# One load for the modulation weights, and TensorE's loop body in seven marked parts with branch hints, in a decode kernel

## The chip, the cores and the metric

The kernel runs on one core of a Trainium2 chip. The metric is the device time of one execution in microseconds. For the kernel before it is the median of three runs. A profile of one execution gives the span from its first to its last instruction, the busy time of each engine and every DMA packet.

## What is computed

A decode step (one token for each of B = 8 sequences, width D = 512) of a block with adaptive layer norm, attention over a key and value cache, and a dense layer:

```
mod = silu(c) @ w_mod                       # 512 x 3072; six parts sa, ca, ga, sb, cb, gb
h = layernorm(x) * (1 + ca) + sa
q = h @ wq                                  # 32 heads of 128
o = softmax(q k^T / sqrt(128)) v            # 8 key/value heads, 8192 positions, per sequence
x = x + ga * (o @ wo)
h = layernorm(x) * (1 + cb) + sb
x = x + gb * (relu(h @ w1 + b1)^2 @ w2 + b2)   # width 1792
```

All inputs are bfloat16. The key and value caches hold 8 x 8 x 8192 x 128 elements each, 134 MB each; everything is read once.

## The kernel before, in words

**The units of the caches.** The caches are read in units of two heads of one sequence, 4 MB each: 128 partitions of 32 KB. A sequence has four key units and four value units, so there are 64 units. They go through `RING`, four slots in SBUF; unit n uses slot n mod 4. `load(n)` (L354 to L367) issues a unit's DMA on SyncE's queue once the slot's last reader, a matmul of TensorE, has run; the last value unit goes in four pieces (L362).

**The start.** SyncE issues, in this order: w_mod into slot 2 (L288, two DMAs: partitions 0 to 15, then 16 to 127), wq into slot 3 (L290), key units 0 and 1 into slots 0 and 1 (L367), the two biases (L451, L452), wo (L453), then key units 2 and 3 as soon as TensorE has read w_mod and wq out of their slots. ScalarE's queue brings c (L284) and x (L285). GpSimd builds constants (L297 to L344). TensorE transposes silu(c) (L375), x (L381) and the normalised x (L394), multiplies by w_mod (L400, 24 matmuls of 512 columns), turns the result (L414, L423), and multiplies the modulated `haT` by wq (L400 again, 32 matmuls). `haT` is written by VectorE after L414.

**The loop.** One pass per sequence, eight passes. A pass does, for each of the four key units and each quarter k of it: 32 transposes of 128 x 128 tiles on TensorE (L481), copies of the results out of PSUM by VectorE (L488) and ScalarE (L486), and eight score matmuls of the quarter before (L498). Then the row maximum, the exponential (L564), the turning of the probabilities (L576), and for each value unit 32 matmuls (L618), a copy (L628) and four small matmuls (L632). A few matmuls on constants (L465, L471) write banks that nobody reads afterwards.

**Who writes the order.** `op` and `dma` append to one list per engine, in the order of the Python text. `Prog._looped` (L126 to L154) writes the list of TensorE, VectorE and ScalarE: first what stands ahead of the loop, then a hardware loop of `passes` passes whose body is written once, with part "a" of every pass and part "b" of all but the last, then what comes after. SyncE's and GpSimd's lists are written out in full. A wait stands in front of an instruction where a token has not been seen by its engine. Part "a" of TensorE's list is numbered j = 0, 1, 2, ... in `_looped`; that number counts matmuls.

**The end.** After the last pass come the output projection (L525, L706), the second layer norm, w1 (L739) and w2 (L753), whose weights are the last loads on SyncE's queue (L659, L661), and the output (L761, L769).

The two DMAs of w_mod, as they stand:

```
wmod_p = w_mod.rearrange("(p k) n -> p (k n)", k=KT)
for a, z in ((0, 16), (16, 128)):
    d_wm = dma("sync", s_wm, lambda e, a=a, z=z: e.dma_start(
        RING[a:z, 2, 0:KT * NMOD], wmod_p[a:z]))
d_wq = dma("sync", s_wq, lambda e: e.dma_start(
    RING[:, 3, :], A_wq.rearrange("(p k) n -> p (k n)", k=KT)))
```

Of the kernel before, what the change touches and what calls it, by code (L numbers as in the profile page):

```python
# [12 lines left out]
class Tok:  # L13
# [4 lines left out]
    def __init__(self, op, at, sem=None, val=None):  # L18
        self.op, self.at, self.sem, self.val = op, at, sem, val


class Op:
# [3 lines left out]
    def __init__(self, eng, fn, deps, sem, at):  # L26
        self.eng, self.fn, self.deps, self.sem, self.at = eng, fn, [d for d in deps if d is not None], sem, at
        self.tok, self.users = None, set()
        for d in self.deps:
            if d.op is not None:  # L30
                d.op.users.add(eng)


class Prog:
# [25 lines left out]
    def dma(self, eng, sem, fn, deps=()):  # L60
        self.dma_n[sem] = self.dma_n.get(sem, 0) + 16
        self.ops[eng].append(Op(eng, fn, deps, sem, self.at))
        return Tok(None, self.at, sem, self.dma_n[sem])
# [61 lines left out]

    def _looped(self, e, eng, passes):  # L126
        nc, per, pe = self.nc, self.per[e], self.LOOP[e]
        seen, first = {}, {}
        for o in self._part(e, None):
            self._emit(eng, o, self._want(e, o, 0), seen)  # L130
        for i in range(passes):
            for p in "ab":
                for j, o in enumerate(self._part(e, (i, p))):
                    want = self._want(e, o, i)
                    inside = {s: v for s, v in want.items() if s in per}
                    assert all(v <= per[s] for s, v in inside.items())
                    assert all(d.at is None or d.sem in per for d in o.deps), (e, i, p, j)
                    assert first.setdefault((p, j), inside) == inside, (e, i, p, j)
                    self._emit(eng, None, {s: v for s, v in want.items() if s not in per}, seen)
        with nc.Fori(0, passes, engines=[pe], head_slot={pe: 0} if e == "tensor" else None) as i:  # L140
            self.batch = i
            for j, o in enumerate(self._part(e, (0, "a"))):
                self._emit(eng, o, first["a", j], seen)
            after = dict(seen)
            with eng.If(i < passes - 1):
                for j, o in enumerate(self._part(e, (0, "b"))):
                    self._emit(eng, o, first["b", j], seen)
                self._emit(eng, None, per, seen)
                eng.drain()
                for s, n in per.items():  # L150
                    eng.sem_inc(s, -n)
            self.batch = None
        for o in self._part(e, "post"):
            self._emit(eng, o, self._want(e, o, passes - 1), after)  # L154
# [14 lines left out]
def bass_adaLN_cond__gqa_block_cached__dense_activation_squared_relu__decode_kernel(  # L169
# [6 lines left out]
    NMOD = w_mod.shape[1]  # L176
    KT = D // 128
# [9 lines left out]
    with ExitStack() as es:  # L187
        E = es.enter_context
        sb = lambda name, shape, dt: E(nc.sbuf_tensor(name, shape, dt))
        RING = sb("ring", [128, NSLOT, UNIT], BF16)  # L190
# [80 lines left out]
        op, dma = Pg.op, Pg.dma  # L271
        sem = lambda name: E(nc.semaphore(name))
        s_c, s_x, s_wm, s_wq, s_wo, s_bb = (
            sem(f"d_{n}") for n in ("c", "x", "wm", "wq", "wo", "bb"))
# [8 lines left out]

        d_c = dma("scalar", s_c, lambda e: e.dma_start(c_sb, c))  # L284
        d_x = dma("scalar", s_x, lambda e: e.dma_start(x_sb, A_x.rearrange("b s d -> (b s) d")))  # L285
        wmod_p = w_mod.rearrange("(p k) n -> p (k n)", k=KT)
        for a, z in ((0, 16), (16, 128)):
            d_wm = dma("sync", s_wm, lambda e, a=a, z=z: e.dma_start(  # L288
                RING[a:z, 2, 0:KT * NMOD], wmod_p[a:z]))
        d_wq = dma("sync", s_wq, lambda e: e.dma_start(  # L290
            RING[:, 3, :], A_wq.rearrange("(p k) n -> p (k n)", k=KT)))

# [238 lines left out]
        for b in range(B):  # L531
# [5 lines left out]
            for p in range(NP):  # L537
                n = 2 * NP * b + p
# [69 lines left out]
            for p in range(NP):  # L608
                if p == NP - 1:
                    Pg.at = "post" if lastb else (b, "b")  # L610
                n = 2 * NP * b + NP + p
# [191 lines left out]
```

## Time and profile before

| what | value |
|---|---|
| median of three runs | 675.81 us (675.12 to 675.97) |
| the profiled execution's own time | 675.12 us |
| its span, first to last instruction | 673.3 us |
| TensorE matmul busy | 517.4 us, 77% of the span |
| TensorE weight load busy | 347.1 us, 52% |
| VectorE busy | 302.5 us, 45% |
| ScalarE busy | 258.9 us, 38% |
| GpSimd busy | 18.6 us, 3% |
| moved by DMA | 283.85 MB, mean 422 GB/s |
| mean granted TensorE clock | 0.888 |

How to read it. Times of single rows come from the profiled execution, whose own time is 1.8 us longer than its span. In the page, the rows of 40 digits cut the span into 40 equal slices (16.8 us each) and give the busy share of an engine in tenths, 9 for 90% or more. A DMA's landing time runs from its issue to the arrival of its completion. In a row of waits, "A <- B: total, times, longest" means that engine and line A stood idle until B was done. "q1" is the queue of SyncE's DMAs, "q10" that of ScalarE's, and a row of kind "instruction" counts DMA packets that bring program code, here in pieces of 16 KB on "q8" and smaller ones on "q14".

### The profile page before, as it was taken

To read this page: it belongs to the slowest core of one execution; us is meant where nothing else is said; L and a number is where in the kernel's file an instruction comes from. 1 tells how busy PE (TensorE), PEld (TensorE's weight loads), DVE (VectorE), ACT (ScalarE), POOL (GpSimd) and SP (SyncE) were. 2 spreads that over 40 slices of the span, in tenths; PEclk is the share of its full clock that TensorE was granted. 3 is DMA by queue.
4 is the path that set the end of the run, shared out by engine and by line. 5 is a ranking of instruction groups with operands and counts; after the bars stand their busy time and mean duration, and the time that the engine had idled before them with its cause. 6 is when DMAs were issued, how large, how long until landed. Compare 5 with 4: busy or idle time off the path is not lost.

```text
span 673.3 us, 15486 instructions
## 1 busy us (share of the span) xinstructions
PE 517.4 (77%) x7064; PEld 347.1 (52%) x7064; DVE 302.5 (45%) x571; ACT 258.9 (38%) x289; POOL 18.6 (3%) x76
## 2 busy tenths in 40 slices
PE   0684986699839986599756998399856998489886
PEld 0373742577318752377316763187424773177534
DVE  1242551367315662267414663066612674156622
ACT  2143560265404661166403662056601664046610
POOL 7300000000000000000000000000000000000000
PEclk9778898699977999699977999789995999689995
DMA  9999999999999999999999999999999999999996
GB/s 233 425 414 434 433 424 433 434 434 432 424 434 432 430 436 432 432 430 428 432 430 436 432 434 432 426 432 428 436 432 434 432 426 432 430 434 432 434 413 265
DMA packets 12192, 283.85 MB, mean 422 GB/s; under 512 B 1266, under 2 KB 1299, under 8 KB 3604
## 3 DMA queue, kind: packets, MB, share of 16 engines
q1 hardware_dynamic: 12132, 283.65, 99.1%
q8 instruction: 9, 0.15, 0.1%
q10 hardware_dynamic: 48, 0.02, 0.0%
q14 instruction: 3, 0.02, 0.0%
HBM read 283.66 MB, written 0.01 MB: 421 GB/s over the span
## 4 chain that ended last, share of the span: by engine, by line
PE 52%; DMA 37%; ACT 7%; DVE 2%; SPq 1%; issue 1%
PE PS L481 36%; DMA ring<-in_A_k_cache_dram 32%; PE PS L498 9%; ACT P_sb L564 5%; DMA ring<-in_A_wq_dram 3%; DMA ring<-in_B_w_dram 2%; PE PS L618 2%; PE PS L471 1%; ACT KTb L486 1%; SPq L661 1%; DVE O_sb L628 1%; PE PS L465 1%; PE PS L576 1%; DVE Pm L590 0%; PE PS L596 0%
## 5 line engine op out<-in xcount | busy, mean ns | idle before, releaser
L486 ACT ACTIVATE KTb<-PS 128x1024 bf16<-128x1024 bf16 x192 | 196.7, 1024 | 331.2 <-PE PS L481 331.2
L481 PE MATMUL PS<-IDENT,ring 128*128 128x128 bf16 x4096 | 269.5, 228 | 49.7 <-DMA ring<-in_A_k_cache_dram 49.7
L481 PEld LDWEIGHTS PS<-IDENT,ring 128*128 128x128 bf16 x4096 | 248.8, 103 | 98.5 <-DMA ring<-in_A_k_cache_dram 50.9
L488 DVE COPY KTb<-PS 128x1024 bf16<-128x1024 bf16 x320 | 210.1, 687 | 145.3 <-PE PS L481 143.1
L618 PE MATMUL PS<-ring,Pm 128*32 128x512 bf16 x992 | 70.8, 435 | 45.3 <-DMA ring<-in_A_v_cache_dram 44.3
L498 PE MATMUL PS<-KTb,Qb 128*32 128x512 bf16 x1024 | 79.2, 386 | 4.5 <-ACT KTb L486 4.5
L628 DVE CAST O_sb<-PS 128x512 bf16<-128x512 f32 x31 | 21.4, 692 | 125.5 <-PE PS L618 125.5
L618 PEld LDWEIGHTS PS<-ring,Pm 128*32 128x32 bf16 x992 | 26.9, 106 | 83.8 <-DMA ring<-in_A_v_cache_dram 52.1
L564 ACT ACTIVATE P_sb<-PS,negm 128x1024 bf16<-128x1024 f32 x32 | 35.2, 1112 | 20.2 <-DVE negm L559 20.2
L471 PE MATMUL PS<-ONES 128*128 128x512 f32 x80 | 42.1, 630 | 0.0
L576 PE MATMUL PS<-IDENT,P_sb 128*128 128x128 bf16 x256 | 19.9, 220 | 15.4 <-ACT P_sb L564 15.4
L590 DVE COPY Pm<-PS 64x512 bf16<-64x512 bf16 x48 | 20.2, 421 | 25.0 <-PE PS L576 24.6
L576 PEld LDWEIGHTS PS<-IDENT,P_sb 128*128 128x128 bf16 x256 | 14.4, 98 | 25.2 <-ACT P_sb L564 25.2
L465 PE MATMUL PS<-IDENT 128*128 128x512 bf16 x88 | 26.9, 380 | 0.0
L498 PEld LDWEIGHTS PS<-KTb,Qb 128*32 128x32 bf16 x1024 | 15.4, 94 | 21.1 <-ACT KTb L486 8.5
L505 DVE TENSOR_REDUCE m<-PS 128x1 f32<-128x512 f32 x32 | 22.0, 689 | 6.6 <-PE PS L498 6.6
L632 PEld LDWEIGHTS PS<-SEL,O_sb 128*128 128x128 bf16 x124 | 5.8, 98 | 30.8 <-DVE O_sb L628 30.8
L471 PEld LDWEIGHTS PS<-ONES 128*128 128x128 f32 x80 | 12.7, 190 | 10.6 <-issue 10.6
L632 PE MATMUL PS<-SEL,O_sb 128*128 128x8 bf16 x124 | 7.9, 169 | 12.4 <-DVE O_sb L628 12.0
L400 PE MATMUL PS<-ring,KTb 128*32 128x512 bf16 x56 | 7.2, 626 | 7.8 <-DMA ring<-in_w_mod_dram 4.6
L643 DVE TENSOR_TENSOR oTn<-PS,rinv 128x8 f32 x31 | 6.0, 194 | 14.9 <-PE PS L632 14.9
L465 PEld LDWEIGHTS PS<-IDENT 128*128 128x128 bf16 x88 | 7.7, 105 | 9.1 <-issue 7.2
(132 smaller groups left out, 120.0 us busy)
## 6 DMA issues: line engine op xcount, KB each, us to landing
ring<-in_A_k_cache_dram SPq DMA_DIRECT2D x32, 4096.0 KB, 34.2
ring<-in_A_v_cache_dram SPq DMA_DIRECT2D x31, 4096.0 KB, 27.4
ring<-in_A_wq_dram SPq DMA_DIRECT2D x1, 4096.0 KB, 25.0
wo_sb<-in_A_wo_dram SPq DMA_DIRECT2D x1, 4096.0 KB, 53.4
ring<-in_w_mod_dram SPq DMA_DIRECT2D x1, 2688.0 KB, 15.7
ring<-in_A_v_cache_dram SPq DMA_DIRECT2D x1, 2048.0 KB, 23.5
ring<-in_B_w_dram SPq DMA_DIRECT2D x3, 512.0 KB, 17.6
ring<-in_B_w_dram SPq DMA_DIRECT2D x1, 1344.0 KB, 18.8
```

The source lines that it names most:

```text
L465: ts = [op("tensor", lambda e: e.matmul(bank(at).rearrange("p (a r) -> p a r", a=4), IDENT[:, :], rhs)) for _ in range(n)]
L471: ts = [op("tensor", lambda e: e.matmul(bank(at).rearrange("p (a r) -> p a r", a=4), ONES[:, :], rhs)) for _ in range(n)]
L481: t = op("tensor", lambda e, j=j, i=i: e.matmul(STG[j][:, i, :], src[:, 32 * k + 8 * j + i, :], IDENT[:, :], is_transpose=True), [loaded[n ...
L486: stg_free[j] = op("scalar", lambda e, j=j, dst=dst: e.activation(dst, STG[j], ACT.Copy), [t])
L488: stg_free[j] = op("vector", lambda e, j=j, dst=dst: e.tensor_copy(dst, STG[j]), [t])
L498: t = op("tensor", lambda e, hf=hf, q=q, rhs=rhs: e.matmul(PS[32 * q:32 * (q + 1), k, :], Qb[:, 2 * p + hf, :], rhs, start=(p == 0 and hf ...
L505: return op("vector", lambda e: e.tensor_reduce(m4[:, k:k + 1], bank(k), AX.X, ALU.max), [t])
L564: exps.append(op("scalar", lambda e, k=k: e.activation(P_sb[:, k, :, :, :], bank(k).rearrange("p (i x) -> p i x", i=8).unsqueeze(2).to_bro ...
L576: t = op("tensor", lambda e, k=k, i=i: e.matmul(STG[k][:, i, :], P_sb[:, k, i, :, :].rearrange("p h x -> p (h x)"), IDENT[:, :], is_transp ...
L590: done.append(op("vector", lambda e, dst=dst, frm=frm: e.tensor_copy(dst, frm), [t, k_pm]))
L618: t = op("tensor", lambda e, p=p, m=m, cg=cg, vt=vt, Obank=Obank: e.matmul(Obank[32 * cg:32 * (cg + 1), :], lhs[:, p, 32 * m:32 * m + 32], ...
L628: t = op("vector", lambda e, osb=osb, Obank=Obank: e.tensor_copy(osb, Obank), [t])
```

## The change

The loads: w_mod comes in one DMA over all 128 partitions in place of two. The program: TensorE's first instructions become seven prefetch hints, each for one branch; and in part "a" of its loop body, ahead of the matmuls with the numbers in `MARK`, stands a branch to the instruction that follows, so that the body is cut by seven branches. Both targets of each branch are the same label; in the built instruction list each is one unconditional branch. The lists of VectorE, ScalarE and GpSimd keep their instructions and their order; SyncE's has one DMA fewer.

```diff
+MARK = (130, 260, 380, 505, 630, 740, 790)
...
     def _looped(self, e, eng, passes):
         nc, per, pe = self.nc, self.per[e], self.LOOP[e]
+        es = ExitStack()
         seen, first = {}, {}
+        marks = [f"pe_part{i}" for i in range(2, 9)] if e == "tensor" else []
+        if marks:
+            r = es.enter_context(eng.register("never"))
+            eng.reg_mov(r, 0)
+            locs = [eng.mark_branch_hint_location() for m in marks]
         for o in self._part(e, None):
             self._emit(eng, o, self._want(e, o, 0), seen)
...
             for j, o in enumerate(self._part(e, (0, "a"))):
+                if marks and j in MARK:
+                    k = MARK.index(j)
+                    m = marks[k]
+                    eng.br_lt(r, 1, on_true=m, on_false=m).branch_hint(locs[k])
+                    nc.switch_bb(m)
                 self._emit(eng, o, first["a", j], seen)
...
-        wmod_p = w_mod.rearrange("(p k) n -> p (k n)", k=KT)
-        for a, z in ((0, 16), (16, 128)):
-            d_wm = dma("sync", s_wm, lambda e, a=a, z=z: e.dma_start(
-                RING[a:z, 2, 0:KT * NMOD], wmod_p[a:z]))
+        d_wm = dma("sync", s_wm, lambda e: e.dma_start(
+            RING[:, 2, 0:KT * NMOD], w_mod.rearrange("(p k) n -> p (k n)", k=KT)))
```

## The prediction

> **What bounds the kernel now.** I read the page's 40 slices first, then stretches by window, then the transfers' landings, then TensorE's waits. The slices:
>
> ```profile
> PE   0684986699839986599756998399856998489886
> DMA  9999999999999999999999999999999999999996
> GB/s 233 425 414 434 433 424 433 434 434 432 424 434 432 430 436 432 432 430 428 432 430 436 432 434 432 426 432 428 436 432 434 432 426 432 430 434 432 434 413 265
> ```
>
> The DMA engines are busy in every slice and move 424 to 436 GB/s nearly everywhere. TensorE has holes. So the bytes set the time: a microsecond won or lost in the DMA stream reaches the end; one of TensorE's does not while it still waits for data. The odd slice is the first: busy, yet 233 GB/s. Windows (columns: stretch, length, busy time of five engines, clock, DMA share, GB/s):
>
> ```profile
> 0.00:1.80 1.80, 0.00 (x0) 0.00 (x0) 0.00 (x0) 0.05 (x1) 1.21 (x15) 1.00 0.08 3
> 1.80:16.00 14.20, 1.19 (x12) 0.93 (x12) 2.62 (x8) 3.35 (x4) 10.98 (x29) 1.00 1.05 257
> 16.00:20.00 4.00, 2.97 (x24) 1.07 (x24) 0.68 (x1) 0.00 (x0) 2.28 (x13) 1.00 0.93 395
> 60.00:350.00 290.00, 225.79 (x3024) 149.39 (x3028) 131.81 (x241) 113.88 (x128) 0.00 (x0) 0.89 1.00 431
> 350.00:640.00 290.00, 234.15 (x3229) 159.91 (x3222) 142.36 (x255) 124.22 (x138) 0.00 (x0) 0.90 1.00 432
> ```
>
> From 1.8 to 16 us the DMA engines are fully occupied at 257 GB/s, against 431 later. What is in flight then is w_mod, as the landings show:
>
> ```profile
> ring<-in_A_wq_dram SPq DMA_DIRECT2D x1, 4096.0 KB, 25.0
> ...
> ring<-in_w_mod_dram SPq DMA_DIRECT2D x1, 2688.0 KB, 15.7
> ...
> ring<-in_w_mod_dram SPq DMA_DIRECT2D x1, 384.0 KB, 5.6
> ```
>
> The 16-row piece is issued at 0.81, the 112-row piece at about 1.26, wq at 1.71. They land at 6.4, 16.96 and 26.71. So wq, one DMA over 128 partitions queued right behind, takes 26.71 - 16.96 = 9.75 us for 4.194 MB: 430 GB/s at once. w_mod's 3.146 MB takes from 1.8 to 16.96: 15.2 us, 207 GB/s. The slowness goes with the split transfer and ends with it.
>
> TensorE's waits in the second pass (103 to 181 us) give its reserve:
>
> ```profile
> PE PS L618 <- DMA ring<-in_A_v_cache_dram: 5.7, 1, 5.7
> PE PS L481 <- DMA ring<-in_A_k_cache_dram: 5.0, 1, 5.0
> ```
>
> It stands still for data 10.7 us a pass. Last, the instruction-fetch queue, over the whole run:
>
> ```profile
> q8 instruction: 9, 0.15, 0.1%
> ```
>
> Seven of the nine lie in 24 to 110 us, the first pass; none between 110 and 650. So the loop, once fetched, stays.
>
> **What the Trainium skill says.** "DMA: Bandwidth & Descriptors", "Why a DMA increments its semaphore by 16 and not by 1": a DMA runs on the largest k up to 16 that divides its slowest dimension. 16, 112 and 128 all give 16 engines, so the split leaves no engine out. Same page, "The descriptor swizzle": over 128 partitions each engine's eight rows all go to one SBUF port, no two engines sharing one; other shapes need not. "SBUF — State Buffer", "Door 1: The DMA port swizzle": four neighbouring partitions share a port, partitions 0 to 15 reach only 4 of 16 ports, and 104 GB/s was measured there. The trace agrees: the 16-row piece, 0.393 MB from 1.8 to 6.4 us, is 85 GB/s with the other piece already behind it. In the 112-row piece seven rows per engine cut across the groups of four, so engines meet at ports: my reading for the 257 GB/s. "Runtime: NRT & Kernel Launch", "Instruction fetch mechanics": a taken branch whose target is not held stalls for a fetch, and only two pages are held. The trace disagrees on the second part: a loop with seven fetches in its first pass needs none in passes 2 to 8.
>
> **The change part by part.**
>
> 1. *w_mod in one DMA of 128 rows.* At 431 GB/s 3.146 MB take 7.3 us in place of 15.2. By the last landing that is up to 7.9 us; part of the 15.2 is the delay from last byte to landing, under 0.8 us, which stays: 7.1. Counted by bytes, which averages the 16 engines: 1.8 to 20 us moved 14.2 x 257 + 4.0 x 395 = 5.23 MB, where 18.2 x 431 = 7.84 MB would fit; 2.61 MB missing are 6.1 us. The end waits for the last engine, and uneven ports leave engines uneven, so the truth lies between. I take 6.7, ends 6.1 and 7.9. All later transfers follow in the same queue, so they move up by this.
>
> 2. *The first DMA has 128 rows, not 16.* Issuing took 0.39 and 0.41 us for w_mod's pieces and 0.42 for wq's 128 rows: 0.03 us longer. Whether bytes start later the trace cannot show: nothing to 0.4 us lost; I take 0. SP issues one DMA fewer, so wq, two k units, the biases and wo are queued 0.4 us sooner, behind at least 7 us of queued w_mod: worth nothing, since it is hidden by the bytes ahead. ACT's queue (c, x) is not passed.
>
> 3. *Work that w_mod's landing released.* L400 began at 17.03. It would now find data at about 9.9, but L394, ahead of it on TensorE, ends at 12.42, after x (landed 9.28, itself held up among w_mod's packets). From L400 to the finished haT took 17.03 to 23.54, 6.5 us; from 12.4 that ends at 18.9, and wq lands at about 19.6. So wq still ends that wait. Then the first k unit: 36.45 becomes about 29.5; GpSimd's last constant, which TensorE awaits before the loop, is ready at 27.05. It fits by 2.4 us. Were it late, SP's queue still holds k, wo and the biases, so the DMA stream would not notice.
>
> 4. *Seven prefetch hints at TensorE's start.* They stand ahead of L375, which waits for VectorE until 5.30: cover of about 4.5 us. If they cost more, part 3's chain loses its margin of 0.7 us and then eats the 9.0 us that TensorE waits for k data near 67 us; still nothing at the end. What they move: seven fetches of 16 KB, each 1.1 us of one DMA engine (13.7% of 16 engines over a half microsecond), out of the full stream: 7 x 1.1 / 16 = 0.48 us on average if they run before 1.8 us, when the DMA engines are idle; nothing if among w_mod's packets. If one falls on an engine that is last anyway, up to 1.1 us either way. I take 0.3 gained, bounds -1.1 and 1.1.
>
> 5. *Seven branches a pass.* The skill's price ("Advanced Engine Details and Errata", "Control Flow Timing") is 51 ns for an unconditional branch, 108 for a compare and branch; the built instruction list shows unconditional ones. No branch row in the trace prices it. 7 x 51 = 0.36 us a pass (0.76 at the dearer price) lies beside 10.7 us of waiting for data: nothing. Released slots come 0.36 us later; loads spend a median 27 to 34 us between issue and landing, about three units of 9.75 us, so the stream does not run dry.
>
> 6. *The tail.* From the last landing (L753 resumes at 669.27) to 673.3 stay 4.0 us. L753's first half started at 667.35 and ran 1.02 us, so TensorE is within 0.9 us of becoming the bound there; more than that could not be gained in the tail alone, but parts 1 and 4 move both.
>
> Sum for the profiled execution, 673.3 of span and 1.8 around it: 675.1 - 6.7 - 0.3 = 668.1. The median of the runs lies 0.7 above that execution: 668.8.
>
> **Rivals.**
>
> A. *One DMA is better but not at the full rate* (first rows slow, a late start, fetches in the way): 2 to 5.5 us gained, about 672. For it: no lone 128-row transfer at the start is seen. Against: wq's 430 GB/s directly behind.
>
> B. *The slowness belongs to the start, not to the split*: only part 4 counts, 675.5. Against it: a warm-up would also slow wq, and the rate does not climb steadily in the window.
>
> C. *The change does not do what it says: the hints bring nothing*, and the first pass fetches as before. Then 6.7 alone: 669.1, inside the forecast's own range.
>
> D. *Slower: the branches leave what is held.* If a branch to the next part forces a fetch every pass, each costs at least the fetch's 1.1 us plus about 1 us from issue to first byte (0.81 to 1.8), at most another 1.2 us for a 32 KB packet ahead of it (32,768 B at 431/16 GB/s): 2.1 to 3.3 us. It decides from 10.7 / 7 = 1.5 us a branch. At 2.1: (14.7 - 10.7) x 7 later passes = 28 us, less 6.7: 697; at 3.3, 756. For it: the skill's two pages. Against: no fetch in passes 2 to 8 now, and the loop grows by only seven branches.
>
> **How the numbers follow.** Forecast with C 0.80 (C alone 0.12), A 0.10, B 0.06, D 0.04. Forecast's own range: 675.8 - 7.9 - 0.5 = 667.4 to 675.8 - 6.1 + 0.4 = 670.1. A reaches to 673.8; taking its better half gives 671.6. Downwards, a lucky last engine (part 4) gives 667.0. What this kernel's measurement can tell from no change is about 0.2%, 1.35 us: faster 0.90 (forecast and A), same 0.06 (B), slower 0.04 (D).
>
> **What would show it.** Right: one w_mod row of 3072 KB landing about 9 us after issue; L400's first wait for wq ending near 19.7; GB/s of the first slice near 380 (431 over 15.0 of its 16.8 us); seven q8 packets before 10 us, none in the first pass; stretches from 60 us on still at 431. Wrong: w_mod still landing after 14 us (B); q8 packets in every pass and TensorE waiting for "issue" at the part borders (D); DMA share below 1.00 in mid-run, which would mean TensorE frees slots too late.

## The result, and the profile after

The changed kernel takes 670.01 us (median of four runs, 669.44 to 670.26), the kernel before 675.67 us (four runs, 675.12 to 675.97): ratio 0.9916, 95% interval 0.9899 to 0.9933. So 5.7 us (0.8%) are gone, where 7.0 were forecast. The profiled execution of the changed kernel took 669.9 us, with a span of 668.1; its span is 5.2 us shorter than that of before.

The 40 slices of the changed kernel, TensorE, DMA and GB/s:

```profile
PE   3395984898739975699838987499766997399885
DMA  9999999999999999999999999999999999999996
GB/s 376 433 406 439 424 434 428 438 424 436 432 436 426 434 432 436 428 432 432 436 434 426 432 436 434 426 434 434 436 426 432 434 438 424 432 434 438 424 418 254
```

Only the first slice is another: 376 GB/s in place of 233. The DMA engines are still busy throughout. The windows of the changed kernel (stretch, length, five busy times, clock, DMA share, GB/s):

```profile
1.80:16.00 14.20, 5.79 (x41) 3.08 (x41) 3.29 (x9) 3.94 (x5) 10.98 (x29) 1.00 1.01 407
16.00:20.00 4.00, 2.83 (x13) 2.65 (x12) 1.08 (x5) 0.00 (x0) 2.28 (x13) 1.00 1.12 483
60.00:350.00 290.00, 225.57 (x3048) 147.41 (x3048) 132.61 (x244) 113.81 (x128) 0.00 (x0) 0.90 1.00 432
350.00:640.00 290.00, 235.41 (x3258) 161.05 (x3262) 143.07 (x257) 126.09 (x140) 0.00 (x0) 0.91 1.00 432
```

From 1.8 to 20 us it moved 14.2 x 407 + 4.0 x 483 = 7.71 MB, where the kernel before moved 5.23 MB. The 2.48 MB more are 5.8 us at 431 GB/s: the whole gain lies in these first 20 us, and from 60 us on the rates are those of before. The landings of the changed kernel (issue in us after start: w_mod 0.81, wq 1.26):

```profile
ring<-in_A_wq_dram SPq DMA_DIRECT2D x1, 4096.0 KB, 20.0
...
ring<-in_w_mod_dram SPq DMA_DIRECT2D x1, 3072.0 KB, 10.6
```

w_mod is there at 11.4 us instead of 16.96, wq at 21.3 instead of 26.7: 5.4 to 5.6 us sooner. At the end the span is 5.2 us shorter and the median 5.7 us, so that lead is kept.

The rest of the change shows too, without reaching the end. Views of the changed kernel: the fetch queue; the hints, the seven branches in the loop body and the loop's own branch (line, sequencer, operation, count: duration in ns least/median/most, first and last start in us; the trace lists every branch as COMPARE_BRANCH); and TensorE's waits from 25 to 103 us:

```profile
q8 instruction: 10, 0.16, 0.1%
```

```profile
L137 PEldq BRANCH_PREFETCH_HINT  x7: 31/31/45, 0.9 to 1.5; - x7
```

```profile
L155 PEldq COMPARE_BRANCH  x56: 163/163/303, 42.4 to 644.5; - x56
```

```profile
L149 PEldq COMPARE_BRANCH  x9: 82/213/6776, 27.6 to 647.4; - x9
```

```profile
PE PS L493 <- issue: 8.5, 1, 8.5
PE PS L493 <- DMA ring<-in_A_k_cache_dram: 6.9, 1, 6.9
```

The hints are issued at 0.9 to 1.5 us and cost 31 ns each. No fetch follows them: the fetch queue brings nothing before 24 us, eight packets from 24 to 110 us (seven before the change) and two at the end. The branch at L149 that leads into the loop once took 6.8 us, from 27.6 us on; in the kernel before its longest was 315 ns. The first of the eight fetches moves at 31.9 us, inside that stall. The first transpose of the loop starts at 34.48 us, though the key unit's data is at hand near 31 us (an estimate: 9.7 us after wq's landing, as in the kernel before). TensorE loses some 3.5 us there and then waits 6.9 us for data at 61.5 us where it waited 9.0 before. The late start is paid out of a wait.

### The profile page after: what moved, and what is told of

It reads as the page before. It is cut to its first block, busy times and chain, and to the rows that moved or that the text cites. A ratio compares the mean times of both kernels' runs of the same rounds, so it can differ in the third digit from the quotient of the medians.

```text
span 668.1 us, 15548 instructions
## 1 busy us (share of the span) xinstructions
PE 513.8 (77%) x7064; PEld 343.9 (51%) x7064; DVE 302.2 (45%) x571; ACT 258.7 (39%) x289; POOL 18.6 (3%) x76
## 4 chain that ended last, share of the span: by engine, by line
PE 52%; DMA 37%; ACT 7%; DVE 2%; SPq 1%; issue 1%
PE PS L493 36%; DMA ring<-in_A_k_cache_dram 32%; PE PS L510 9%; ACT P_sb L576 5%; PE PS L630 2%; DMA ring<-in_B_w_dram 2%; DMA ring<-in_A_wq_dram 2%; SPq L673 1%; PE PS L483 1%; ACT KTb L498 1%; DVE O_sb L640 1%; PE PS L477 1%; PE PS L588 1%; DVE Pm L602 0%; PE PS L608 0%
## 5 line engine op out<-in xcount | busy, mean ns | idle before, releaser
L493 PE MATMUL PS<-IDENT,ring 128*128 128x128 bf16 x4096 | 265.6, 227 | 51.3 <-DMA ring<-in_A_k_cache_dram 42.9
L493 PEld LDWEIGHTS PS<-IDENT,ring 128*128 128x128 bf16 x4096 | 245.1, 102 | 99.7 <-DMA ring<-in_A_k_cache_dram 44.0
L483 PEld LDWEIGHTS PS<-ONES 128*128 128x128 f32 x80 | 12.7, 190 | 10.6 <-issue 10.6
## 6 DMA issues: line engine op xcount, KB each, us to landing
ring<-in_w_mod_dram SPq DMA_DIRECT2D x1, 3072.0 KB, 10.6
```

Of the source, the lines that this page charges most:

```text
L483: ts = [op("tensor", lambda e: e.matmul(bank(at).rearrange("p (a r) -> p a r", a=4), ONES[:, :], rhs)) for _ in range(n)]
L493: t = op("tensor", lambda e, j=j, i=i: e.matmul(STG[j][:, i, :], src[:, 32 * k + 8 * j + i, :], IDENT[:, :], is_transpose=True), [loaded[n ...
```

## The experiments

The theory, P: the row split made DMA engines meet at SBUF ports, and its end is the whole gain. Rivals: H, hints and branches bring part of the gain (or cost some); B or S, the stream is slow at its start, or where two DMAs stand for one, whatever the rows.

| run | w_mod, wq | hints, branches | us | ratio to before, 95% interval |
|---|---|---|---|---|
| before | 16 + 112 rows | none | 675.57 | |
| changed, again | 128 rows | 7, 7 | 669.75 | 0.9910 (0.9894 to 0.9927) |
| one load | 128 rows | none | 669.38 | 0.9909 (0.9894 to 0.9924) |
| hints only | 16 + 112 rows | 7, 7 | 675.70 | 1.0004 (0.9996 to 1.0013) |
| two by columns | 2 x 128 rows | none | 669.60 | 0.9913 (0.9898 to 0.9928) |
| 64 + 64 | 64 + 64 rows | none | 677.47 | 1.0028 (1.0017 to 1.0039) |
| wq split | 128 rows, wq 16 + 112 | none | 680.17 | 1.0064 (1.0047 to 1.0081) |
| wq first | wq, then w_mod, 128 rows | none | 669.56 | 0.9910 (0.9893 to 0.9926) |
| hints late | 128 rows | 7 before the loop, 7 | 669.62 | 0.9909 (0.9892 to 0.9925) |
| one hint, last mark | 128 rows | 1, 1 | 669.88 | 0.9920 (0.9904 to 0.9937) |
| no hints, condition always true | 128 rows | 0, none in the trace | 669.35 | 0.9910 (0.9894 to 0.9927) |
| conditional branches | 128 rows | 0, 7 conditional | 669.73 | 0.9917 (0.9900 to 0.9933) |
| one hint, first mark | 128 rows | 1, 1 | 669.39 | 0.9910 (0.9893 to 0.9926) |

The kernel before was timed beside each group, and each ratio is to its own group: 675.57 beside one load, hints only, two by columns and 64 + 64; 675.63 beside changed again, wq split, wq first and hints late; 675.45 beside the last-mark hint and the always-true condition; 675.62 beside the conditional branches and the first-mark hint.

**One part each.** One load, nothing else:

```diff
-        wmod_p = w_mod.rearrange("(p k) n -> p (k n)", k=KT)
-        for a, z in ((0, 16), (16, 128)):
-            d_wm = dma("sync", s_wm, lambda e, a=a, z=z: e.dma_start(
-                RING[a:z, 2, 0:KT * NMOD], wmod_p[a:z]))
+        d_wm = dma("sync", s_wm, lambda e: e.dma_start(
+            RING[:, 2, 0:KT * NMOD], w_mod.rearrange("(p k) n -> p (k n)", k=KT)))
```

> The kernel before with w_mod in one DMA of 128 rows; no hints, no branches. Theory P (the whole gain is the row split's: rows cut at 16 make DMA engines meet at SBUF ports): 670.0 us like the changed kernel, within 0.7; w_mod lands 10.6 us after its issue, the loop begins right after the first key unit's landing near 31 us, 7 instruction fetches in the first pass. Theory H (hints and branches bring part of it): slower than the changed kernel by 0.3 to 0.5 us, with w_mod landing alike. If hints and branches cost something at the end of the stream (one more fetch, the late start of the loop at 34.5 us): up to 1 us faster than the changed kernel.

669.38 us: the whole gain, 6.2 us. Seven fetches lie in the first pass, and its landings are:

```profile
ring<-in_A_wq_dram SPq DMA_DIRECT2D x1, 4096.0 KB, 19.6
...
ring<-in_w_mod_dram SPq DMA_DIRECT2D x1, 3072.0 KB, 10.2
```

Hints only is the changed kernel with the same lines reversed:

> The changed kernel with w_mod in its two DMAs of 16 and 112 rows again; hints and branches stay. Theory P: 675.7 us, as before, within 0.7; the 112-row piece lands 15.7 us after issue. Theory H: 675.2. The loop's first transpose would come some 3 us after the first key unit's landing if the hints are what delays it, and right at it if the delay came from the earlier landing.

675.70 against 675.57: no difference that can be measured. Its windows are those of before (257 GB/s from 1.8 to 16 us), its fetches eight and two, as in the changed kernel. So the two halves separate: the load is the gain, and hints and branches change nothing that can be measured. Its loop did begin late, at 37.87 us, 1.4 us after the kernel before (some 3 us had been expected): the branch into the loop took 5.2 us.

**Why two DMAs were slow: the number, or the rows?**

```diff
-        for a, z in ((0, 16), (16, 128)):
+        for a, z in ((0, 6144), (6144, 12288)):
             d_wm = dma("sync", s_wm, lambda e, a=a, z=z: e.dma_start(
-                RING[a:z, 2, 0:KT * NMOD], wmod_p[a:z]))
+                RING[:, 2, a:z], wmod_p[:, a:z]))
```

> The kernel before, w_mod still in two DMAs but cut by columns: each piece 128 rows of 12 KB. Theory P: no slower than one DMA: second piece lands about 10.2 to 10.6 us after the first one's issue, time 670.0 within 0.7. Rival S (two DMAs, or the start of the stream, are what is slow): w_mod lands near 17 us, time 675.5.

669.60 us, and the second piece landed 10.2 us after the first one's issue. Its window:

```profile
1.80:16.00 14.20, 6.20 (x44) 3.65 (x44) 3.37 (x9) 3.94 (x5) 10.89 (x29) 1.00 1.01 407
```

Two DMAs are as good as one when each has all 128 rows. Then rows cut in the middle:

```diff
-        for a, z in ((0, 16), (16, 128)):
+        for a, z in ((0, 64), (64, 128)):
```

> The kernel before, w_mod in two DMAs of 64 rows. Theory P: each half reaches only 8 of 16 ports, so two engines share each port: 3.146 MB at about 218 GB/s are 14.4 us, the second half lands near 17 us, time 675.7 to 676.7. Rival (only the little 16-row piece on 4 ports, or seven rows per engine, is what is slow; even halves are fine): w_mod lands near 11.5, time 670.5.

677.47 us, beyond the upper end of what P had said, and slower than before by 0.28% (0.17 to 0.39). The window of this kernel:

```profile
1.80:16.00 14.20, 1.20 (x12) 0.94 (x12) 2.62 (x8) 3.35 (x4) 10.90 (x29) 1.00 1.02 217
```

217 GB/s with fully busy DMA engines is half of 431 to within a per cent. The Trainium skill's "SBUF — State Buffer", "Door 1: The DMA port swizzle", gives partitions 0 to 63 eight of the sixteen ports and an asymptote of about 218 GB/s, the figure that P used. The DMA packets of the traces show the same from nearer. A row of w_mod is one packet of 24 KB; its median time is 0.91 us with one load, 1.51 with 16 + 112 rows and 1.92 with 64 + 64, where nearly every packet takes twice as long. So even halves are the worst of the cuts tried for w_mod.

What is shown is that cutting the rows is slow. That the engines meet at SBUF ports is P's reading of it: the 217 GB/s and the doubled packets are what two engines to a port would give, but no run parts a row's place in SBUF from its place in DRAM.

**The place in the stream.** wq split, w_mod whole:

```diff
+        wq_p = A_wq.rearrange("(p k) n -> p (k n)", k=KT)
+        for a, z in ((0, 16), (16, 128)):
+            d_wq = dma("sync", s_wq, lambda e, a=a, z=z: e.dma_start(RING[a:z, 3, :], wq_p[a:z]))
-        d_wq = dma("sync", s_wq, lambda e: e.dma_start(
-            RING[:, 3, :], A_wq.rearrange("(p k) n -> p (k n)", k=KT)))
```

> w_mod in one DMA, and wq in two DMAs of 16 and 112 rows instead. Theory P (row split makes engines meet at ports, whatever the tensor and wherever in the stream): wq now runs at about 210 to 260 GB/s behind a fast w_mod; its excess is that of w_mod's split scaled by 4/3 in bytes, 7 to 8 us: 676 to 677.5 us. Rival B (the start of the stream is slow, not the split): about 670, wq landing about 20 us after issue.

680.17 us: the slowness went with the split, as P says, and B falls. The size was a miss, by some 3 us. In this kernel's trace the landings and the window are:

```profile
ring<-in_A_wq_dram SPq DMA_DIRECT2D x1, 3584.0 KB, 31.1
ring<-in_w_mod_dram SPq DMA_DIRECT2D x1, 3072.0 KB, 13.5
```

```profile
14.00:33.00 19.00, 6.62 (x44) 4.06 (x48) 1.76 (x6) 0.60 (x1) 7.39 (x39) 0.71 0.93 233
```

The rate, 233 GB/s, is in the range that P named. What its sum left out is that w_mod itself is held up: it landed 13.5 us after its issue, against 10.2 with wq whole. The packets show where: wq's first 16 rows, which begin at 9.98 us, take 3.5 to 4.7 us each in place of 1.21, and the packet of w_mod that starts among them takes 2.6 us in place of 0.91. That those rows crowd the few ports of partitions 0 to 15 would explain both; no run took that apart.

**The start.** wq issued ahead of w_mod, both whole:

```diff
+        d_wq = dma("sync", s_wq, lambda e: e.dma_start(
+            RING[:, 3, :], A_wq.rearrange("(p k) n -> p (k n)", k=KT)))
         d_wm = dma("sync", s_wm, lambda e: e.dma_start(
             RING[:, 2, 0:KT * NMOD], w_mod.rearrange("(p k) n -> p (k n)", k=KT)))
-        d_wq = dma("sync", s_wq, lambda e: e.dma_start(
-            RING[:, 3, :], A_wq.rearrange("(p k) n -> p (k n)", k=KT)))
```

> One load each for w_mod and wq, wq issued first. Theory: each engine's first packet costs a fixed 0.6 to 0.8 us more than its size, whatever the tensor: wq's first 32 KB packets take about 1.9 us instead of 1.2, w_mod's none more than 0.95; the pair lands as late as in the other order (near 21 us), time 669.4 within 0.7. Rival (w_mod's own place or rows are slow to start): wq's first packets take 1.2 us and the pair lands 0.7 us sooner.

669.56 us. The landings of this kernel, wq issued at 0.81, w_mod at about 1.26:

```profile
ring<-in_A_wq_dram SPq DMA_DIRECT2D x1, 4096.0 KB, 12.6
...
ring<-in_w_mod_dram SPq DMA_DIRECT2D x1, 3072.0 KB, 19.5
```

wq, now first, needs from 1.8 to 13.4 us: 11.6 us for what takes 9.7 at 431 GB/s, 1.9 us more. w_mod, now second, follows in 20.76 - 13.4 = 7.35 us: 428 GB/s. With w_mod first (one load), it takes from 1.8 to 11.0, 1.9 us more than its 7.3, and wq follows in 9.8. So whichever comes first pays 1.9 us over its bytes, up to the signal of its landing, and the second pays nothing. That is a price of the first transfer, not of w_mod. The packets bear the expectation out: the first sixteen of wq take a median of 1.88 us in place of 1.21, and those of w_mod, now second, 0.91; with w_mod first its first sixteen take 1.59. So some 0.7 us of the 1.9 are the engines' first packets. About 0.3 us lie between the end of the last packet and the landing (10.69 to 11.01 us with one load); the rest was not taken apart.

**What the hints did.** The changed kernel, timed once more:

> The changed kernel itself, to set beside the kernel with one load and no hints (669.38 us). If hints and branches cost something: 670.0, about 0.6 above that. If the difference was chance in one engine's start: 669.4.

669.75 us; the eight runs of it lie between 669.34 and 670.26, those of one load alone between 669.32 and 669.40. The medians are 0.4 to 0.6 us apart, 0.1%, and come from different groups; single runs with one hint, or with branches and no hint, reach 670.2 to 670.4 too. So a cost of the hints is neither shown nor ruled out. The hints issued right ahead of the loop:

```diff
-            locs = [eng.mark_branch_hint_location() for m in marks]
...
+        if marks:
+            locs = [eng.mark_branch_hint_location() for m in marks]
         with nc.Fori(0, passes, engines=[pe], head_slot={pe: 0} if e == "tensor" else None) as i:
```

> The changed kernel with its seven hints issued right ahead of the loop instead of as TensorE's first instructions. Theory (the hints, once issued, take the place of the fetch of the following block, so the loop's first block is missing when TensorE gets there): with hints late, that block has been fetched before, and the loop begins at the first key unit's landing, near 30.7 us. Rival (the branches or the loop's size make it miss): it begins near 34.5 us as in the changed kernel. Time 669.4 to 670.0 in both.

That theory fell: the hints ran at 27.2 to 27.8 us, the branch into the loop took 7.4 us all the same, and the first transpose came at 35.51 us. One mark only, the last and the first:

```diff
-MARK = (130, 260, 380, 505, 630, 740, 790)
+MARK = (790,)
...
-        marks = [f"pe_part{i}" for i in range(2, 9)] if e == "tensor" else []
+        marks = [f"pe_part{i}" for i in range(2, 3)] if e == "tensor" else []
```

> The changed kernel with only the last of its seven marks: one hint as TensorE's first instruction, one branch. If any hint leads to the late start of the loop: first transpose near 34.4 us and one fetch more than the seven of the first pass. If it is the sum of seven, or the early targets: first transpose near 30.7 us, seven fetches. Time 669.4 to 669.8.

```diff
-MARK = (130, 260, 380, 505, 630, 740, 790)
+MARK = (130,)
```

> The changed kernel with only its first mark (130): one hint, one branch. If one hint to a near target is enough to push the loop's first block out: the branch into the loop takes several us, first transpose near 34.4 us, eight fetches in the first pass. If it takes several hints: under 0.4 us, near 30.7 us, seven fetches. Time 669.4 to 669.9.

Both began at the landing (30.89 and 30.85 us), with seven fetches and a branch into the loop of at most 0.36 us. Branches without hints:

```diff
-            locs = [eng.mark_branch_hint_location() for m in marks]
...
-                    eng.br_lt(r, 1, on_true=m, on_false=m).branch_hint(locs[k])
-                    nc.switch_bb(m)
+                    with eng.If(i < passes):
+                        eng.reg_mov(r, 0)
```

> One load for w_mod, and at the seven marks an unconditional branch without hints (each behind a register move in a condition that always holds). If the hints make the loop's first block late: first transpose near 30.7 us as with one load alone. If the branches or the loop's length do: near 34.4 us. In both: no instruction fetch between 110 and 650 us, and 669.4 us, since 7 branches a pass lie beside TensorE's waiting for data.

669.35 us, first transpose at 30.87. But the trace has no row for these branches, so this run is one load with seven register moves and tells nothing of branches. With `i < passes - 1` as the condition they stay:

> One load for w_mod, no hints, and at the seven marks a real compare and branch around one register move, since the unconditional ones of the run before left no row in the trace. If the hints delay the loop's entry: its branch takes under 0.4 us and the first transpose comes near 30.7 us. If branches in the body do: near 34.4 us, with one row of several us for the branch into the loop. Time 669.4 in both: 7 branches of under 0.3 us a pass lie beside some 11 us of waiting for data.

In that kernel the branches are there and the loop's entry is not late. First its marks in all passes, then those before and after 590 us, then the line that enters the loop:

```profile
L152 PEldq COMPARE_BRANCH  x56: 65/65/210, 39.2 to 644.6; - x56
```

```profile
L152 PEldq COMPARE_BRANCH  x49: 65/65/86, 39.2 to 566.8; - x49
```

```profile
L152 PEldq COMPARE_BRANCH  x7: 202/202/210, 594.9 to 644.6; - x7
```

```profile
L148 PEldq COMPARE_BRANCH  x9: 76/209/315, 27.1 to 647.5; - x9
```

The first transpose came at 30.91, the time is 669.73. The condition `i < passes - 1` holds in the first seven passes, so 49 of the 56 branches fall through, at 65 ns, and only the seven of the last pass are taken, at 202 ns. So the loop's first branch stalls, and an eighth fetch comes, in all four traces with seven hints and their branches; one hint with its branch, near or far, does not do it, nor do seven branches that fall through. Seven taken branches without hints were not run, so that rival stands; how many hints it takes, and whether they push the loop's first block out of what TensorE holds, is open too. The late start does not reach the end.

## Why the prediction was right, point by point

**The bound.** Right. All kernels here have 431 or 432 GB/s in mid-run, and what changed the time changed the first 33 us of the DMA stream. In the changed kernel the first landings came 5.4 to 5.6 us sooner, and the span ended 5.2 us sooner.

**The sum.** Of the 7.0 us forecast 5.7 came. With one load alone 6.2 came, so 0.5 of the 1.3 missing are Part 1's; 0.3 are Part 4's; the other 0.5 lie between the changed kernel and one load and are not explained. The time is only 0.1 us inside the upper end of the forecast's own range (670.1), and that end holds 0.4 us for a later first byte, which did not come. So the number owes something to luck; the sign and the cause do not. Two ends of the wider range do not follow from the figures given with them: A's better half (3.75 us gained or more) ends at 672.05, not 671.6, and a gain of 7.9 with Part 4's bound of 1.1 at 666.8, not 667.0. Nothing rests on them.

**Part 1, w_mod in one DMA.** That the row cut is the cause was right and is shown: rows cut at 16 or at 64 are slow, columns are not, and the slowness moves with the cut to another tensor. That engines meet at ports fits the 217 GB/s and the packet times and is not shown by itself. The size was the term that was off: 6.7 us with ends 6.1 and 7.9. Alone it measured 6.2 us by the medians and 5.9 at the landings; in the changed kernel the landings gave 5.4 to 5.6. The step that mis-sized it is "At 431 GB/s 3.146 MB take 7.3 us in place of 15.2", counted from 1.8 us, with under 0.8 us of delay to the landing. With one load w_mod took 9.2 us, 1.9 over its bytes, and runs with either tensor first show that the first transfer pays this whatever it is. So 1.1 us more than the 0.8 allowed could not be won by any change of rows, and had been booked as the split's. In this kernel's profiled execution w_mod landed 0.4 us later still than with one load alone (10.6 against 10.2 us after issue); in another profile of the same kernel it was 10.2, so this part varies between executions. The count by bytes, 6.1, was the better of the two measures, and the right choice was its end of the range.

**Part 2, 128 rows in the first DMA.** Right at nothing for the issue (0.39 us as before) and for the first bytes: the windows are empty up to 1.8 us in both kernels.

**Part 3, the work behind w_mod.** Right in its outcome. x arrived earlier too: L393 began at 8.12 instead of 9.29 us, so TensorE stood ready at 11.25 and w_mod's landing, not x, released L412 at 11.40. The forecast had x's chain last, by 2.5 us; w_mod, later than forecast, came last by 0.15. wq's landing (L412 again at 21.43, forecast 19.6) still ended the next wait. The loop, forecast for about 29.5, began at 30.64 with one load and at 34.48 in the changed kernel; that the DMA stream would not notice a late start was right.

**Part 4, the hints.** Wrong in what they do, harmless in what they cost. What was to move out of the full stream, "seven fetches of 16 KB", did not: the fetches came at TensorE's pace in the first pass, and one more than before. Rival C stands in this part. The forecast gave them 0.3 us of gain; alone they measured 675.70 against 675.57, an interval from 0.3 us gained to 0.9 us lost. The cover that was named, the 9.0 us of waiting for key data near 67 us, held: the branch into the loop took 6.8 us, and that wait shrank to 6.9 us.

**Part 5, the branches.** Right at nothing, at three times the price. The rows show a median of 163 ns for the 56, against 51 in the Trainium skill's "Advanced Engine Details and Errata", "Control Flow Timing" (108 for a compare and branch, under which name the trace lists them). For the conditional branches above, which have no hint, being taken or not makes the difference: 202 ns against 65. 7 x 163 = 1.1 us a pass lie beside waits for data of 11.5 us in the second pass of the changed kernel:

```profile
PE PS L630 <- DMA ring<-in_A_v_cache_dram: 6.5, 1, 6.5
PE PS L493 <- DMA ring<-in_A_k_cache_dram: 5.0, 1, 5.0
```

**Part 6, the tail.** The last wait for data (L765, 0.51 us, to 664.68) still ends it, 3.4 us ahead of the end, where 4.0 were to stay: the last landing came 4.6 us sooner than before, and 0.6 us fell off the tail, within the 0.9 that the prediction named.

**The signs and the rivals.** Of the signs named, the first slice's 376 GB/s (near 380) and 432 in mid-run came; w_mod's landing took 10.6 us (about 9), and the seven packets before 10 us did not come. B fell by wq's split and by the order of the two. D did not come: no fetch between 110 and 640 us. The prediction let the trace disagree with two held pages. It passed over another figure of the same section of the Trainium skill, "Runtime: NRT & Kernel Launch", "Instruction fetch mechanics": the store is 128 KiB for TensorE, or eight of its 16 KiB blocks. Seven blocks that stay agree with that, and the section spoke less for D than the prediction had it. That a taken branch can stall for a fetch, as the section has it, did show, once, at the loop's entry: 6.8 us where the median of that line is 0.2. D's price per branch (2.1 to 3.3 us) was below that; at such a price in every pass D would have been worse than stated. A named the right sign of the miss, a first transfer that starts slowly, though the time stayed inside the forecast's own range.

## What to carry to other kernels

In a stream that is DMA-bound from the first byte, a load's shape counts as much as its bytes: keep all 128 partitions in each DMA, and if a load must come in pieces cut its columns. A stretch with DMA engines fully busy and GB/s at a half to two thirds of the rest is the sign to look for. When the cost of a first transfer is read off its landing, take the price of starting from another transfer put first before the remainder is booked as gain.

## What the runs showed of the hardware that had not been expected

- The first transfer of the program costs 1.9 us over its bytes at 431 GB/s, from the first packet to the landing's signal, for w_mod as for wq; the second costs nearly nothing over (426 to 428 GB/s from landing to landing). Some 0.7 us of it is that each engine's first packet takes longer (1.88 us in place of 1.21 for 32 KB).
- Two 64-row DMAs of w_mod run at 217 GB/s, a 24 KB packet taking a median of 1.92 us in place of 0.91, and 64 + 64 rows are slower than 16 + 112 by 1.9 us here.
- Seven branch prefetch hints take 31 ns each and, issued 26 us or a fraction of a microsecond ahead of the loop, are followed by no early fetch, but, with their seven branches, by a branch into the loop of 5.2 to 7.4 us and one fetch more. One hint with its branch has none of this.
- On TensorE's sequencer a hinted branch to the next instruction takes 163 ns. Without a hint, a compare and branch around one register move takes 65 ns when it falls through and 202 ns when it is taken; the loop's own takes a median of 213 ns (the changed kernel).
